# Normalizing the first block early and in two column parts, loading wk ahead of x blocks 2 and 3, and re-ranking the task order, in a fused attention + MLP kernel

## The chip, the cores and the metric

The kernel runs on one core of one Trainium2 chip. The metric is device microseconds (us) of that core. TensorE does the matrix products, VectorE (DVE in the profile) and ScalarE (ACT) the elementwise work, GpSimd (POOL) a few helpers, and SyncE (SP) issues most transfers. The profile calls TensorE "PE". The span is the stretch that the profile covers; the time is about 2 us longer than the span. A transfer has landed when its data is there. PSUM is the memory that TensorE writes its products to; it is used here in banks, which the other engines read.

## The reference, cut to what matters

```python
xn = layernorm(x)                      # x: 2048 rows of 640
return x + A(xn) + B(xn)

# A: q, k, v = xn @ wqkv; 32 heads of 20; each row looks at 8 earlier rows, 2 apart;
#    softmax over the 8; output @ wo
# B: gelu(xn @ w1 + b1) @ w2 + b2      # 640 -> 1536 -> 640
```

All operands are bf16.

## The kernel before

The rows are worked in four chunks of 512, each of four blocks of 128. The program doesn't write its instructions in a fixed order. It describes some hundreds of tasks (name, engine, modelled duration, rank, needs, buffers), and a small list scheduler runs a model of the clock: whenever an engine is free, it takes the ready task of the lowest rank. The order that comes out is the order in which each engine's queue is filled, and each engine then works its queue in that order. `RANK` holds offsets to the ranks, found by search.

```python
RANK = {
    "ad02": 53.9, "ad11": 29.1, "av2": -13.3, "f11": 8.8, ...   # cut
}
    for n, ...:                                  # n: the chunk; bl: the block in it
        pl.add(f"st{n}{bl}", VE, 1.17, ...)      # statistics, both halves and the aggregate
        pl.add(f"rs{n}{bl}", SE, 0.35, ...)      # square root        (chunk 0: by block)
        pl.add(f"rc{n}{bl}", VE, 0.17, ...)      # reciprocal
        pl.add(f"xn{n}{bl}", ...)                # normalized block: DVE in chunk 0, ScalarE later
        pl.add(f"tp{n}{bl}", PE, 0.3, ...)       # chunk 0: five transposes into a PSUM bank
        pl.add(f"tc{n}{bl}", SE, 0.65, ...)      # ... and the copy to xnT
        pl.add(f"gj{bl}{g}", PE, ...)            # chunk 0: projections block by block, 4 of 128 columns in one bank
        pl.add(f"pj{n}{which}{to}", PE, 1.08, ...)   # chunks 1 to 3: projections of 512 columns
        pl.add(f"pc{n}{which}{to}", SE, 0.52, ...)   # their copies out of PSUM (qT, kT, vT)
        pl.add(f"xs{n}", SE, 1.2, [f"at{n}"], f("xs", n), [at, ax])   # two DMA issues on ScalarE
        pl.add(f"xd{n}", DQ, 6.0, [f"at{n}"], f("xd", n), [at, ax])   # two DMA issues on SyncE
        # cut: qk, lg, max ... at (attention weights), av, ad, ot (weighted sums),
        #      f1, ge (first MLP product, gelu), o, oc (second product, output)
```

The loads are all issued by SyncE but for block 1 of x:

```python
    nc.sync.dma_start(x_sb[:, 0, :], x_nb[:, 0, :])
    nc.scalar.dma_start(x_sb[:, 1, :], x_nb[:, 1, :])
    for s in range(3):                                        # wq, wk, wv
        nc.sync.dma_start(wqkv[s][:], wqkv_v[:, :, s * D : (s + 1) * D])
        if s == 0:
            nc.sync.dma_start(x_sb[:, 2:BPC, :], x_nb[:, 2:BPC, :])
    # cut: b1, x of chunks 1 to 3, w1
```

Four transfers spread `attn` over the partitions of `ax`. Two are issued by SyncE and two by ScalarE, so they stand in ScalarE's queue among its copies:

```python
    def expand(queue, n, blocks):
        ax = get(("ax", n), lambda: axp.tile([P, BPC, W, P], BF16, tag="ax", name="ax"))
        for j in blocks:
            queue.dma_start(ax[:, j, :, :], tiles["attn", n][j * H : (j + 1) * H, :, :]...)   # cut
    def do_xd(n): expand(nc.sync, n, (0, 1))
    def do_xs(n): expand(nc.scalar, n, (2, 3))
```

`ax` has one buffer, so the issue for a chunk waits until DVE has read `ax` of the chunk before for the last time (the `pv` products). Projections and gelu inputs share four PSUM banks (tag "acc"), and a bank comes free when ScalarE (for `b1T`, DVE) has copied it out.

Names in the profile: `gps` are the projections of chunk 0, `pps` those of the later chunks, `hps` the first MLP product, `lo` and `hi` the output product, `L` the attention logits, `idle` the warm-up.

## Time and profile before

| | before |
|---|---|
| time, median of 6 runs | 215.12 us (215.06 to 216.11) |
| span of the profiled run | 212.9 us |
| TensorE busy | 206.1 us, 97% |
| first projection matmul (`gps`) | 7.70 us |
| first matmul on wk | 9.93 us |
| first `hps` matmul: all 300 projections of chunk 0 are done | 25.32 us |
| end of the last matmul | 210.10 us |

The last four rows are read from the start times in the trace. They cut the run into the start (until 25.3), the long middle, and the tail. Where holes are compared below, they are distances from one matmul's start to the next, less the usual step of that shape, with suspected missing records set aside.

### The profile page before, as it was taken

The numbers are of one execution on the slowest core, as the hardware profiler recorded it, in microseconds if no ns is written. First come the engines' busy times: TensorE is split into PE (matmuls) and PEld (weight loads), VectorE is DVE, ScalarE is ACT, GpSimd is POOL, SyncE is SP. The second block draws the span as 40 slices with busy tenths as digits, with TensorE's granted clock in tenths as the row PEclk, the third lists the DMA queues.
The fourth block names the chain that finished last, engine by engine and source line by source line (L and its number), as shares of the span: only waits on it lengthen the run. The fifth ranks groups of instructions, "written<-read, shape, count | busy, mean of one in ns | idle before, by whom it ended". The sixth has DMA issues, their size and how long they took to land.

```text
span 212.9 us, 3943 instructions
## 1 busy us (share of the span) xinstructions
PE 206.1 (97%) x1665; PEld 121.2 (57%) x1690; DVE 174.2 (82%) x176; ACT 106.8 (50%) x190; POOL 19.5 (9%) x36
## 2 busy tenths in 40 slices
PE   7899999999999999999999999999999999999994
PEld 7799844654544556556555555554555455555552
DVE  2849999459999999999999999999499789982001
ACT  3567899689565733635428273420297321351210
POOL 2000000000011015101001010110101011101220
PEclk9999999999999999999999999999999999999999
DMA  6999417973939579977002180211021822202223
GB/s 211 364 363 381 78 31 198 386 67 41 228 115 140 76 261 211 197 115 190 0 3 31 17 210 4 31 7 27 2 31 14 216 32 31 26 8 32 34 31 62
DMA packets 23433, 23.95 MB, mean 112 GB/s; under 512 B 9080, under 2 KB 20600, under 8 KB 23416
## 3 DMA queue, kind: packets, MB, share of 16 engines
q1 hardware_dynamic: 17832, 16.49, 28.0%
q0 software_dynamic: 4144, 4.92, 17.3%
q10 hardware_dynamic: 1440, 2.29, 3.7%
q8 instruction: 13, 0.21, 0.4%
q14 instruction: 4, 0.03, 0.0%
HBM read 10.00 MB, written 7.54 MB: 82 GB/s over the span
## 4 chain that ended last, share of the span: by engine, by line
PE 95%; DMA 1%; DVE 1%; issue 1%; ACT 0%
PE lo L668 26%; PE hps L637 24%; PE pps L472 23%; PE gps L489 8%; PE hi L670 8%; PE L L541 4%; DMA x_sb<-in_A_x_dram 1%; PE tp L429 0%; DVE stats L388 0%; DVE stats L389 0%; ACT xnT L433 0%; DVE xn L415 0%; DVE mv L390 0%; DVE osb L698 0%; PE b_tp L369 0%
## 5 line engine op out<-in xcount | busy, mean ns | idle before, releaser
L637 PE MATMUL hps<-xnT,w_sb 128*128 128x512 bf16 x236 | 53.9, 379 | 0.3 <-issue 0.2
L668 PE MATMUL lo<-w_sb,hT 128*128 128x512 bf16 x186 | 52.6, 379 | 0.0
L615 DVE TENSOR_TENSOR pv<-vT,ax 128x2560 bf16<-128x2560 bf16 x32 | 45.9, 1484 | 4.9 <-PE L L541 2.9
L522 DVE TENSOR_TENSOR prod<-qT,kT 128x2560 bf16<-128x2560 bf16 x32 | 45.5, 1484 | 0.0
L670 PE MATMUL hi<-w_sb,hT 128*128 128x128 bf16 x192 | 40.3, 219 | 0.3
L648 ACT ACTIVATE hT<-hps,b1T 128x512 bf16<-128x512 f32 x48 | 31.4, 687 | 17.0 <-PE hps L637 13.7
L637 PEld LDWEIGHTS <-w_sb 128*128 128x128 bf16 x240 | 22.8, 98 | 26.8 <-issue 0.4
L675 ACT CAST osb<-lo 128x512 bf16<-128x512 f32 x15 | 8.8, 585 | 50.9 <-PE hi L670 22.9
L624 DVE TENSOR_TENSOR pv<-pv 128x5120 bf16<-128x5120 bf16 x12 | 33.9, 2822 | 0.3
L668 PEld LDWEIGHTS <-hT 128*128 128x128 bf16 x192 | 18.7, 98 | 22.6 <-issue 0.2
L681 POOL DMA_DIRECT2D out_dram<-osb x15 | 12.9, 862 | 110.4 <-ACT osb L676 110.4
L668 PE MATMUL lo<-wo,oT 128*128 128x512 bf16 x74 | 22.1, 379 | 0.1
L670 PEld LDWEIGHTS <-hT 128*128 128x128 bf16 x192 | 18.4, 98 | 1.9
L670 PE MATMUL hi<-wo,oT 128*128 128x128 bf16 x80 | 16.9, 219 | 0.3
L472 PE MATMUL pps<-xnT,wk_sb 128*128 128x512 bf16 x71 | 16.9, 380 | 0.2
L472 PE MATMUL pps<-xnT,wq_sb 128*128 128x512 bf16 x72 | 16.9, 380 | 0.2
L472 PE MATMUL pps<-xnT,wv_sb 128*128 128x512 bf16 x73 | 16.9, 379 | 0.1
L689 DVE TENSOR_TENSOR osb<-lo,xlast 128x512 bf16<-128x512 f32 x1 | 0.7, 690 | 16.1 <-PE lo L668 16.1
L507 ACT CAST kT<-pps 128x512 bf16<-128x512 f32 x15 | 8.8, 584 | 8.8 <-PE pps L472 8.6
L668 PEld LDWEIGHTS <-oT 128*128 128x128 bf16 x80 | 7.8, 98 | 9.4
L472 PEld LDWEIGHTS <-wk_sb 128*128 128x128 bf16 x75 | 8.6, 118 | 7.5 <-issue 0.4
L472 PEld LDWEIGHTS <-wv_sb 128*128 128x128 bf16 x75 | 8.6, 117 | 7.2
(63 smaller groups left out, 208.2 us busy)
## 6 DMA issues: line engine op xcount, KB each, us to landing
w_sb<-in_B_w_dram SPq DMA_DIRECT2D x2, 1920.0 KB, 11.5
out_dram<-osb POOLq DMA_DIRECT2D x15, 160.0 KB, 3.4
ax<-attn SPq DMA_DIRECT2D x8, 256.0 KB, 5.1
ax<-attn ACTq DMA_DIRECT2D x8, 256.0 KB, 5.5
x_sb<-in_A_x_dram SPq DMA_DIRECT2D x3, 640.0 KB, 11.4
out_dram<-x_sb SPq DMA_DIRECT2D x3, 640.0 KB, 4.7
out_dram<-b2bc POOLq DMA_DIRECT2D x3, 640.0 KB, 7.7
wq_sb<-in_A_wqkv_dram SPq DMA_DIRECT2D x1, 800.0 KB, 4.9
```

The lines of the kernel that those rows point to most:

```text
L472: nc.tensor.matmul(ps[:], lhsT=wqkv_p[which][:, ti, to, :], rhs=xnT[:, ti, :], start=(ti == 0), stop=(ti == KT - 1),)
L489: nc.tensor.matmul(ps[:, i, :], lhsT=wqkv_p[which][:, ti, to, :], rhs=tiles["xnT", 0][:, ti, cs], start=(ti == 0), stop=(ti == KT - 1),)
L507: nc.scalar.copy(dest[:, to, off : off + CH], tiles["pps", n, which, to][:])
L522: nc.vector.tensor_tensor(out=prod[:, i, :, :], in0=qkv_tile(n, 0)[:], in1=qkv_tile(n, 1)[:, :, off : off + CH], op=ALU.mult,)
L615: nc.vector.tensor_tensor(out=pv[:, i, :, :].rearrange("p t (j c) -> p t j c", j=BPC), in0=qkv_tile(n, 2)[:, :, off : off + CH].rearrange( ...
L624: nc.vector.tensor_tensor(out=ta[:], in0=ta[:], in1=tb[:], op=ALU.add)
L637: nc.tensor.matmul(ps[:], lhsT=w1_sb[:, ti, ft * P : (ft + 1) * P], rhs=tiles["xnT", n][:, ti, :], start=(ti == 0), stop=(ti == KT - 1),)
L648: nc.scalar.activation(hT[:], tiles["hps", n, ft][:], ACT.Gelu_apprx_tanh, bias=b1T[:, ft : ft + 1], scale=1.0)
L668: nc.tensor.matmul(lo[:], lhsT=lhs, rhs=rhs[:, 0:CH], start=first, stop=last)
L670: nc.tensor.matmul(hi[:, 0 : D - CH], lhsT=lhs, rhs=rhs[:, CH:D], start=first, stop=last)
L675: nc.scalar.copy(osb[:, 0:CH], tiles["lo", n, bl][:])
L681: nc.gpsimd.dma_start(rows, tiles["osb", n, bl][:], accum_op=ALU.add)
```

## The change

The intent is to let TensorE begin sooner. Block 0's reciprocal comes ahead of block 1's second statistics; block 0 is normalized, transposed and copied in parts of 256 and 384 columns, so that its first group of projections can start on the first part; and wk, which is needed next, is loaded ahead of x blocks 2 and 3. The ranks were searched anew. The core of the diff:

```diff
-WARM = 40
+WARM = 44
 RANK = {
-    "ad02": 53.9, "ad11": 29.1, "av2": -13.3, "f11": 8.8, ...  (all 22 entries)
+    "ad02": 95.4, "av0": 25.5, "f10": 32.8, ... "rc0": 137.9, "st2": 91.4, "st3": 144.1, "xn0": -16.4,  (again 22 in all)
...
-            pl.add(f"st{n}{bl}", VE, 1.17, -40 if n else -99, [], f("st", n, bl), after=land)
+            pl.add(f"st{n}{bl}a", VE, 0.5, r, [], f("st", n, bl, 0), after=land)
+            pl.add(f"st{n}{bl}", VE, 0.62, r, [f"st{n}{bl}a"] + ([f"rc{n}{bl - 1}"] if n == 0 and bl else []), f("st", n, bl, 1))
...
+            for i, (a, b) in enumerate(((0, 2), (2, KT)) if bl == 0 else ((0, KT),)):
+                pl.add(f"xn{n}{bl}{u}", VE, ..., f("xn", n, bl, a, b), [xn])
+                pl.add(f"tp{n}{bl}{u}", PE, ..., f("tp", n, bl, a, b), [xn, tp])
+                pl.add(f"tc{n}{bl}{u}", SE, ..., f("tc", n, bl, a, b), [tp, xnT])
...
+                    if bl == 0 and g == 0:
+                        cut = 2
+                        need.append(pl.add("ga00", PE, 0.112 * tos, r, ["tc00a"], f("gj", bl, g, 0, cut), [xnT, ps], land))
...
     for s in range(3):
         nc.sync.dma_start(wqkv[s][:], wqkv_v[:, :, s * D : (s + 1) * D])
-        if s == 0:
+        if s == 1:
             nc.sync.dma_start(x_sb[:, 2:BPC, :], x_nb[:, 2:BPC, :])
...
+    zeros = consts.tile([P, P], BF16, name="zeros")
+    nc.vector.memset(zeros[:], 0.0)
...
-            nc.tensor.matmul(idle[:, 0:P], lhsT=ident[:], rhs=ident[:], start=True, stop=True)
+            nc.tensor.matmul(idle[:, 0, :], lhsT=zeros[:], rhs=zeros[:], start=True, stop=True)
```

Left out here: the task functions that take the column range, the start flag that is set once for the split group, the scheduler's modelled landing times, and the last residual add, which works in `x_sb` in place of a tile of its own.

## The prediction

> **What bounds the kernel now.** I read the page first: busy shares and the chain by engine.
>
> ```profile
> PE 206.1 (97%) x1665; PEld 121.2 (57%) x1690; DVE 174.2 (82%) x176; ACT 106.8 (50%) x190; POOL 19.5 (9%) x36
> ...
> PE 95%; DMA 1%; DVE 1%; issue 1%; ACT 0%
> ```
>
> TensorE (PE) is busy for 206.1 of 212.9 us and carries 95% of the chain, so a change helps only where it removes TensorE idle time or TensorE work. To find the idle time I asked for the busy time between the first real matmul (7.70) and the last one (210.10).
>
> ```profile
> 7.70:210.10 202.40, 200.94 (x1615) 116.48 (x1639) 170.22 (x164) 104.00 (x185) 18.21 (x19) 1.00 0.49 108
> ```
>
> The second number is the stretch, the third PE's busy time: 1.46 us idle in 202.40, spread over many small holes. After the end there are 2.8 us of tail (the last add, 0.29 us, and the store), which the change does not touch. What is left is the start, so I read the chain there, in order of time (start, length, what).
>
> ```profile
> 0.74 3.02 DMA x_sb<-in_A_x_dram
> ...
> 4.70 0.21 DVE mv L390
> 4.91 0.36 DVE stats L388
> 5.27 0.40 DVE stats L389
> ...
> 5.69 0.21 DVE mv L390
> 5.90 0.04 DVE rstd L398
> ...
> 5.96 0.46 DVE xn L415
> ...
> 6.47 0.47 PE tp L429 x5
> ...
> 6.96 0.70 ACT xnT L433
> ```
>
> Block 0 of x has landed at 3.76 and its statistics are done at 4.91. The chain then runs through the statistics of block 1 (0.36 + 0.40 + 0.21) before block 0's reciprocal. ScalarE's square root is not the holder, as its row in the timeline shows; it is over at 5.24.
>
> ```profile
> 4.95 0.29 ACT L394 ACTIVATE std<-mv,eps_t 128x1 f32<-128x1 f32 x1 [2.25 <-DVE mv L390]
> ```
>
> Last I read when the weights land (KB, us from issue to landing), because a TensorE that starts sooner asks for them sooner.
>
> ```profile
> wq_sb<-in_A_wqkv_dram SPq DMA_DIRECT2D x1, 800.0 KB, 4.9
> wk_sb<-in_A_wqkv_dram SPq DMA_DIRECT2D x1, 800.0 KB, 7.4
> ...
> x_sb<-in_A_x_dram SPq DMA_DIRECT2D x1, 320.0 KB, 5.3
> ```
>
> Their issues start at 1.20, 2.23 and 1.67 in the timeline, so wq lands at 6.10, x blocks 2 and 3 at 6.97, wk at 9.63. The first wk matmul is at 9.93, after 40 wq matmuls that fill 7.70 to 9.93 (55.7 ns each). So wk is 0.3 us early today: it is the next wait in line.
>
> **What the Trainium skill says.** "TensorE: Matmul & The Clock Gate", Part 1, says the array runs at half clock until a window of about 3.4 us was busy, and falls back after an idle window of that length; 107 ns against 56 ns for 128 columns. The trace agrees: ten warm-up matmuls take the first 1.01 us, and the real ones run at 55.7 ns from 7.70. "DMA: Bandwidth & Descriptors", Queues, rings and completion order, says each DMA engine consumes the descriptors of one queue in ring order; here wq, x 2/3 and wk land in the order of their issue. "VectorE: DVE Perf Modes", The TRN2 errata, says every instruction pays a fixed latency, so splitting costs. The trace has it for ScalarE's PSUM reads: 585 ns for 512 columns and 275 for 128 give 0.81 ns a column plus 0.17 us. "PSUM — Partial Sum Buffer", The four PSUM rules, says a start flag clears the written bits of a whole bank. That is why the split group, whose four slots share one bank, gets one start flag only; the number of matmuls stays. No run shows this yet.
>
> **The change part by part.**
>
> *Reciprocal ahead of block 1's second half.* The square root ends at 5.24, block 1's first half of statistics (start 4.83, 0.44) at 5.27. So the reciprocal can start at about 5.30 instead of 5.82, and xn at 5.44 instead of 5.96 (0.14 later, as now). Gain on this chain: 0.52.
>
> *Two column parts, 256 and 384 of 640.* A DVE operation on one column takes 0.11 to 0.15 and xn on 640 takes 0.446, so about 0.11 plus 0.52 ns a column: 0.25 and 0.31. Part a: xn 5.44 to 5.69; two transposes from 5.75 to 6.03 (one 56 ns step plus 0.219 for the last); the copy, 0.17 + 256 x 0.81 ns = 0.38, to 6.43; the first matmul at 6.47. Part b: xn until 5.95, three transposes until 6.35, its copy (0.17 + 384 x 0.81 ns = 0.48) behind part a's, 6.43 to 6.91. The 8 matmuls of part a take 8 x 55.7 ns = 0.45, until 6.92, so the 12 others follow at about 6.95. The group is through at 6.95 + 12 x 55.7 ns = 7.62. Today it is through at 7.70 + 20 x 55.7 ns = 8.81. Gain at this point: 1.19 us.
>
> *What TensorE does next.* Here I expect most of it to be lost. Block 1 is later than before: its second statistics start after xn b at about 5.95 and end at 6.67 with the aggregate; the square root waits for ScalarE's copy until 6.93, ends at 7.23; reciprocal and xn until 7.87; transposes until 8.2; copy until about 9.0. Block 0's other groups need wk. wk moves to third in the queue. From wq's 6.10, 819 KB at the 365 GB/s of these slices (the window 7.70 to 9.93 shows 369) take 2.24, so 8.34 by rate. Today's 1147 KB behind wq come 0.39 later than the same rate gives (9.63 against 9.24), so 8.3 to 8.75; I take 8.5. TensorE then stands from 7.62 to 8.5 but for block 1's five transposes (0.28), which are over before. Today the state "20 matmuls and block 1's transposes done" is reached at 8.81. What is left: 8.81 - 8.5 = 0.3 us, between 0.05 and 0.5.
>
> *x blocks 2 and 3 later.* They land at today's 9.63, as the bytes ahead of them are then the same. From 8.5 TensorE has k, q+k of block 0 (30 matmuls) and q, k, q+k of block 1 (50): 80 x 55.7 ns = 4.5 us, until 13.0, and v of both (50 more, 2.8 us) after wv's 11.84. Block 2 needs from landing to the end of its copy what block 0 needs today less its wait of 0.52: 7.66 - 3.76 - 0.52 = 3.4 us, so it is there at 13.0. Hidden, with 2.8 us of v work to spare.
>
> *Warm-up.* It waits for GpSimd's identity until 1.49; a zeroed tile on the idle DVE can be there about 0.5 us sooner (the first queues start at 0.74, small instructions take 0.1 to 0.2). 44 matmuls at 107 ns until the clock comes, then 56, end at about 5.5, against 5.75 now: free, and it keeps the array warm over the holes.
>
> *Reordered rest.* The new ranks reshuffle the matmuls after 26 us, with the same count. The 1.46 us of holes is all that they can win; a wait that they open can cost as much. I give this a gain of 0.1 with a spread of 0.5. The last add's in-place x is off the path: the DVE stood 16.1 us before the final add.
>
> Sum: 0.3 + 0.1 = 0.4 us of 215.1.
>
> **The rivals.** *The whole 1.2 us arrives.* That needs wk by about 7.6. Against it: 365 GB/s in all slices, no slack in the queue. With it: 213.8. *wk binds fully, or the hole of a microsecond at 7.6 and the idle before cools the clock.* A hole of 0.72 us today (5.75 to 6.47) does not cool it; if it happened, some 60 matmuls would take 107 instead of 56 ns, 3 us, so 218. *A new stall in the reshuffled middle or end.* DVE has 170.22 of the 202.40 us, and its last attention work ends at 193.15, only 3 us before the group of matmuls at 196.35 that reads the last oT; today the group of 190.10 holds that oT's buffer for 0.85 us. If the order delays attention by more than its slack, TensorE stands for 0.5 to 1.5 us: 215.5 to 216.5.
>
> **Range and chances.** The start gives 0.05 to 0.5, the order -1 to +1. Together 214.7, eight in ten between 213.8 and 215.5. Over 2% faster would be 4.3 us: the start's full 1.2 and all holes of 1.46 make 2.7, so 1%. Over 2% slower needs the cooled clock or a bad stall: 2%.
>
> **What would show it.** Right: reciprocal near 5.3, first projection matmul near 6.5, then a hole before the first wk matmul, which starts near 8.5 with wk's landing; the stretch from there to the last matmul nearly as long as today's. Wrong: no hole after the 20 wq matmuls (wk earlier than I worked out, or other work in between), TensorE waiting for oT or L later on, or matmuls at 107 ns after 7 us. If holes after 26 us shrink or grow by more than 0.5 us, the ranks and not the start decided.

## The result, and the profile after

The changed kernel took 216.56 us (median of 6 runs, 216.08 to 216.89), against 215.12 before. A ratio here is always the mean time of one kernel's fast runs over the mean of the other's fast runs of the same rounds, so it isn't quite the ratio of the medians. It is 1.0057, with a 95% interval of 1.0035 to 1.0080. A difference under 2% counts as "the same" here, but it is slower by about 1.2 us, outside the predicted range of 213.8 to 215.5, and on the other side of the time before than predicted.

| read from start times | before | after | difference |
|---|---|---|---|
| first `gps` matmul | 7.70 | 6.87 | -0.83 |
| first matmul on wk | 9.93 | 8.77 | -1.16 |
| first `hps` matmul | 25.32 | 25.23 | -0.09 |
| end of the last matmul | 210.10 | 211.16 | +1.06 |

So the start did begin earlier, nearly all of that was gone at 25 us, and the loss of about 1.15 us arose after it. The page of the changed kernel shows busy shares first and then the chain by engine:

```profile
PE 208.7 (98%) x1694; PEld 121.9 (57%) x1694; DVE 174.0 (81%) x178; ACT 109.3 (51%) x193; POOL 19.6 (9%) x36
...
PE 75%; DVE 16%; DMA 3%; ACT 2%; ACTq 1%; issue 1%; SPq 0%; DVEq 0%
```

TensorE's share in the chain fell from 95% to 75%. The chain now leaves TensorE somewhere and runs through DVE, a ScalarE DMA issue ("ACTq") and ScalarE before it comes back. It is not that DVE got more work (174.0 against 174.2).

**The start** is as predicted in its outline. The chain of the first 9.5 us (start, length, what) has one long piece, the landing of wk:

```profile
1.67 7.05 DMA wk_sb<-in_A_wqkv_dram
...
8.77 0.75 PE gps L505 x10
```

And the timeline there (start, length, engine, line, operation, shapes, count; in brackets the engine's idle time before it and what ended that):

```profile
4.69 0.30 ACT L406 ACTIVATE std<-mv,eps_t 128x1 f32<-128x1 f32 x1 [2.00 <-DVE mv L402]
5.02 0.16 DVE L410 RECIPROCAL rstd<-std 128x1 f32<-128x1 f32 x1
...
5.66 0.75 PE L439 MATMUL tp<-ident,xn 128*128 128x128 bf16 x5
...
6.45 0.75 ACT L443 COPY xnT<-tp 128x256 bf16<-128x256 bf16 x2 [1.46 <-PE tp L439]
6.87 1.28 PE L505 MATMUL gps<-xnT,wq_sb 128*128 128x128 bf16 x20 [0.46 <-ACT xnT L443]
...
8.13 0.45 PE L439 MATMUL tp<-ident,xn 128*128 128x128 bf16 x5
```

The reciprocal comes right behind the square root. The copy of part a starts only at 6.45, when all five transposes are through, and not after the first two. TensorE then has block 0's 20 wq matmuls and block 1's transposes, and waits 0.19 us for wk.

**The middle** is where the loss is. TensorE's list of waits (total, times, longest) of the kernel before and then of the one after:

```profile
PE tp L429 <- DVE xn L415: 0.7, 1, 0.7
PE gps L489 <- ACT xnT L433: 0.2, 1, 0.2
PE hps L637 <- issue: 0.2, 1, 0.2
```

```profile
PE pps L486 <- ACT vT L524: 0.8, 1, 0.8
PE gps L505 <- ACT xnT L443: 0.5, 1, 0.5
PE gps L505 <- DMA wk_sb<-in_A_wqkv_dram: 0.2, 1, 0.2
```

One wait is new and isn't in the start: projections of a later chunk wait 0.8 us, once, for a `vT` copy of ScalarE. ScalarE's timeline around it, in the kernel after:

```profile
80.23 0.25 ACT L531 COPY kT<-kT 128x70 bf16<-128x70 bf16 x1
81.35 2.37 ACTq L616 DMA_DIRECT2D ax<-attn  x2
83.81 1.56 ACT L524 CAST vT<-pps 128x512 bf16<-128x512 f32 x3 [3.33 <-PE pps L486]
```

and TensorE's there:

```profile
84.45 2.32 PE L486 MATMUL pps<-xnT,wv_sb 128*128 128x512 bf16 x10 [0.82 <-ACT vT L524]
```

ScalarE has its last copy done at 80.5. The next entry of its queue is not a copy but the two issues of chunk 1's `ax` transfers. They wait for DVE's last read of `ax`, which ends at 81.32, and then take 2.37 us. The first `vT` copy behind them starts at 83.81. TensorE meanwhile fills the four "acc" banks and stands: the step from the matmul before to the one at 84.45 is 1.04 us instead of 0.06, so 0.98 are lost. The bracket at 83.81 names "PE pps" as what ended ScalarE's idle time, because issuing isn't counted as busy; the line above shows what really held it.

The same issue held ScalarE as long before. ScalarE's timeline of the kernel before, and TensorE's:

```profile
91.61 0.58 ACT L507 CAST vT<-pps 128x512 bf16<-128x512 f32 x1 [0.49 <-PE pps L472]
92.89 2.34 ACTq L599 DMA_DIRECT2D ax<-attn  x2
95.27 0.58 ACT L675 CAST osb<-lo 128x512 bf16<-128x512 f32 x1 [3.08 <-PE pps L472]
```

```profile
93.58 2.32 PE L472 MATMUL pps<-xnT,wq_sb 128*128 128x512 bf16 x10
95.84 1.28 PE L541 MATMUL L<-prod,head_of 128*32 128x256 bf16 x40
```

In that order it isn't in the way: TensorE had the output product, two projection tiles and the logits to work on, which lie in other banks or in free ones, and its list of waits has none for a ScalarE copy there. So neither the transfer nor its issue is new. Only its place in the queue is.

A second, smaller hole of the same kind is at 128.8 in the kernel after (one `hps` step of 0.407 us instead of 0.216, so 0.19), behind the issue of chunk 2 at 126.07 to 128.43. The sum -0.09 + 0.98 + 0.19 is +1.08, and the end of the last matmul moved by +1.06.

### The profile page after: what moved, and what is told of

The parts are those of the page before. It is cut to its first block, busy times and chain, and to the rows that moved or that the text cites. A ratio compares the mean times of both kernels' runs of the same rounds, so it can differ in the third digit from the quotient of the medians.

```text
span 213.9 us, 3979 instructions
## 1 busy us (share of the span) xinstructions
PE 208.7 (98%) x1694; PEld 121.9 (57%) x1694; DVE 174.0 (81%) x178; ACT 109.3 (51%) x193; POOL 19.6 (9%) x36
## 4 chain that ended last, share of the span: by engine, by line
PE 75%; DVE 16%; DMA 3%; ACT 2%; ACTq 1%; issue 1%; SPq 0%; DVEq 0%
PE lo L685 27%; PE hps L654 19%; PE pps L486 11%; PE gps L505 7%; PE hi L687 7%; DVE pv L632 5%; DVE prod L539 5%; PE L L558 3%; DMA wk_sb<-in_A_wqkv_dram 3%; DVE pv L641 1%; DVE attn L606 1%; ACTq L616 1%; DVE rs L601 1%; DVE sums L596 1%; DVE sums L594 1%
## 5 line engine op out<-in xcount | busy, mean ns | idle before, releaser
L685 PE MATMUL lo<-w_sb,hT 128*128 128x512 bf16 x192 | 53.7, 379 | 0.0
L685 PEld LDWEIGHTS <-hT 128*128 128x128 bf16 x192 | 18.7, 98 | 22.7 <-issue 0.6
L685 PE MATMUL lo<-wo,oT 128*128 128x512 bf16 x80 | 23.2, 379 | 0.0
L400 DVE BATCH_NORM_STATS2 stats<-x_sb 128x6 f32<-128x320 bf16 x32 | 14.0, 469 | 5.2 <-DMA x_sb<-in_A_x_dram 5.2
L486 PE MATMUL pps<-xnT,wk_sb 128*128 128x512 bf16 x75 | 17.4, 380 | 0.0
L706 DVE TENSOR_TENSOR osb<-lo,x_sb 128x512 bf16<-128x512 f32 x1 | 0.7, 692 | 16.1 <-PE lo L685 16.1
L467 POOL DMA_DIRECT2D out_dram<-b2bc x4 | 5.3, 1334 | 88.0 <-DMA out_dram<-x_sb 88.0
```

The source lines that it names most:

```text
L400: nc.vector.bn_stats(stats[:, i, :], x_sb[:, b, i * (D // 2) : (i + 1) * (D // 2)])
L486: nc.tensor.matmul(ps[:], lhsT=wqkv_p[which][:, ti, to, :], rhs=xnT[:, ti, :], start=(ti == 0), stop=(ti == KT - 1),)
L685: nc.tensor.matmul(lo[:], lhsT=lhs, rhs=rhs[:, 0:CH], start=first, stop=last)
```

## The experiments

Every kernel gave the right result. Runs of one group share a chip and the runs of the kernel before (chip 1 in the first group, 15 in the second and third, 9 in the fourth). A comparison between groups is one across chips or rounds; the kernel before took 215.34 to 215.39 in all of them. "Holes" are worked out from start times in the trace, as above.

### First group: is it the issue on ScalarE?

My theory was the queue: the issue on ScalarE, ahead of copies that TensorE needs. The rivals were that the load order or the start does it, and that TensorE just waits for DVE. Before took 215.39 on this chip (median of 11).

**The changed kernel again**, unchanged, as the yardstick.

> The changed kernel as it is, as the control of this chip. Theory and rivals alike: 216.1 to 216.9 us, 1.004 to 1.008 of the kernel before. The trace shows a hole of 0.98 us in the matmuls near 83.4 us and one of 0.19 near 128.8.

It took 216.82 (216.59 to 217.16, 5 runs), ratio 1.0067 (1.0055 to 1.0079). The holes of 0.96 at 83.88 and 0.22 at 129.24 were there again. So was a third, of 0.61 at 14.67, which the first profile didn't have; it is taken up in the second group. The runs of the result had spans of 213.8 to 213.9 (three, the profiled one among them) and of 214.4 (three), so that this hole may sit in half of them; only e0's profile shows it.

**The issues of chunks 1 and 2 moved to SyncE:**

```diff
-        expand(nc.scalar, n, (2, 3))
+        expand(nc.sync if n in (1, 2) else nc.scalar, n, (2, 3))
```

> The changed kernel, with the two expanding DMAs that ScalarE issues in blocks 1 and 2 issued by the sync queue instead; TensorE's and DVE's order is untouched. Theory (ScalarE stands 3.3 us in its queue at those issues, and TensorE's four PSUM banks fill up meanwhile): both holes go, 0.98 + 0.19 = 1.17 us, so 215.2 to 215.5, within 0.2% of the kernel before. Rival A (TensorE waits for ScalarE's copies as such, there are too many of them there): the holes stay, 216.4. Rival B (the later landing of the expanded weights holds up DVE instead): the holes at 83 and 128 go, others come with a wait of L632 for a DMA, and the time stays above 216.

It took 215.13 (214.59 to 215.19, 6 runs), ratio 0.9985 (0.9973 to 0.9998): 1.69 us less than the unchanged one. The order of instructions on TensorE, DVE and ScalarE is the same in both traces (1694, 178 and 193 of them). The time is a little under the expected 215.2 to 215.5. ScalarE's timeline, then SyncE's and TensorE's:

```profile
80.43 0.25 ACT L531 COPY kT<-kT 128x70 bf16<-128x70 bf16 x1
81.63 1.07 ACT L524 CAST vT<-pps 128x512 bf16<-128x512 f32 x2 [0.95 <-DVE pv L632]
```

```profile
81.55 4.22 SPq L616 DMA_DIRECT2D ax<-attn  x4
```

```profile
83.66 2.32 PE L486 MATMUL pps<-xnT,wv_sb 128*128 128x512 bf16 x10
```

The four issues take SyncE 4.22 us, and nothing waits for it. The `vT` copy comes at 81.63, and the matmuls at 83.66 wait for nothing. Both holes are gone. The copy still waits 0.95 us for DVE's `pv`, which reads `vT` of two chunks ago, so it was not the wait for DVE that cost the time but the 2.4 us of issuing behind it: the rival "TensorE waits for DVE" falls.

Of the 1.69 us the span explains some 1.2 (214.4 to mostly 213.2). The other 0.5 lie outside the span; see the third group.

**The issue of chunk 1 left on ScalarE, but behind the next three `vT` copies:**

```diff
+        order = make_plan(fns).run()
+        late = order.pop([t["name"] for t in order].index("xs1"))
+        order.insert([t["name"] for t in order].index("pc222") + 1, late)
```

> The changed kernel, with ScalarE's two issues of block 1 moved in its order behind the next three copies of vT, still on ScalarE. Theory: only the place of the issue was wrong; the hole near 83.4 (0.98) closes and the one near 128.8 (0.19) stays: 215.4 to 215.7. Rival A (too many copies): the hole stays or moves by a few us, 216.4. Rival B (block 1's products wait for the transfer): DVE's first L632 of block 1 moves, 216 or more.

It took 215.58 (215.09 to 215.96, 6 runs), ratio 1.0008 (0.9992 to 1.0024), and the hole at 83 is gone, with the same issue on the same engine:

```profile
82.51 0.59 ACT L524 CAST vT<-pps 128x512 bf16<-128x512 f32 x1 [0.34 <-PE pps L486]
82.65 2.67 ACTq L616 DMA_DIRECT2D ax<-attn  x2
```

So it is its place in the queue and not that ScalarE issues. The six runs lie in two heaps, 215.1 to 215.3 (the profiled one among them) and 215.9 to 216.0; no trace of the second was taken.

**x blocks 2 and 3 ahead of wk again**, all else as changed:

```diff
-        if s == 1:
+        if s == 0:
```

> The changed kernel with the old order of the loads, x blocks 2 and 3 ahead of wk; nothing else. Theory (wk's landing ends the start, so the earlier first matmul is worth nothing by itself): the first wk matmul moves from 8.77 to about 9.7 and the time rises by 0.9 us, to 217.3, unless later holes take it up. Rival (the start does not bind, other slack hides it): no change, 216.4.

It took 217.32 (216.83 to 219.77, 6 runs), ratio 1.0107 (1.0071 to 1.0143). The first wk matmul came at 9.30, not at the expected 9.7. The direction is as expected, but the size, 0.5, is smaller than the spread of these runs (219.77 is one with a mean clock of 0.992), and in the two profiles the start ends at about the same time: the first `hps` comes at 25.76, against 25.69 in e0, which has the hole of 0.61 that this one hasn't. So this run doesn't show that the new load order helps; the fourth group comes back to it.

### Second group: the third hole, the two parts, and whether the ranks did it

Before took 215.34 on this chip (median of 11; one run at 217.62 had a mean clock of 0.992).

The third hole, in DVE's timeline of the changed kernel's second profile, with TensorE's line:

```profile
14.71 0.49 DVE L400 BATCH_NORM_STATS2 stats<-x_sb 128x6 f32<-128x320 bf16 x1 [2.18 <-DMA x_sb<-in_A_x_dram]
...
15.12 0.15 DVE L382 CAST b1T<-b_tp 128x12 f32<-128x12 bf16 x1
...
15.33 0.25 PE L505 MATMUL gps<-xnT,wq_sb 128*128 128x128 bf16 x1 [0.44 <-DVE b1T L382]
```

DVE stands 2.18 us for chunk 1's x, and only then makes the small copy `b1T`, which frees a PSUM bank that TensorE wants. In the kernel before, `b1T` was ahead of these statistics (at 12.47). In the changed kernel's first profile x landed 1 us sooner, and the same order cost nothing. That is a loss that comes and goes with a landing time.

**The issues on SyncE, and chunk 1's first statistics behind the task that makes `b1T`:**

```diff
+        first = order.pop([t["name"] for t in order].index("st10a"))
+        order.insert([t["name"] for t in order].index("gj03") + 1, first)
```

> The kernel of e1 (changed kernel, expanding DMAs of blocks 1 and 2 on the sync queue), and DVE's order altered in one place: the first half statistics of the second chunk, which wait for its x to land, are moved behind the small copy of b1. Theory: that copy frees a PSUM bank; in the changed kernel it stands behind a landing that came at 13.7 us in one profile and at 14.7 in another, where TensorE then stood 0.6 us. So the time is 215.0, up to 0.2 below e1's 215.1, and no hole appears near 14 us in any profile. Rival (the 0.6 us hole was chance and costs nothing on the mean): same as e1 within 0.1.

It took 214.88 (214.51 to 216.39, 6 runs), ratio 0.998 (0.9942 to 1.0017). The hole at 14 us is gone, but its profile has another, of 0.64 at 18.7:

```profile
19.42 0.45 PE L439 MATMUL tp<-ident,xn 128*128 128x128 bf16 x5 [0.47 <-DVE xn L426]
```

Block 3's reciprocal and `xn` stand behind all of chunk 1's statistics. It's the same fault one step later: work that waits for a late transfer is ahead of work that TensorE needs. The third group mends it.

**The same with block 0 in one part:**

```diff
     def do_xn(n, bl, a=0, b=KT):
+        if n == 0 and bl == 0:
+            if a:
+                return
+            b = KT
```

(and likewise in the transposes and the copy)

> The kernel of e4 with block 0's normalization, transposes and copy in one part again, every other instruction in its place. Theory (wk's landing ends the start, and the copy of the first part waits for all five transposes anyway): first projection matmul at about 7.2 instead of 6.9, wk's first matmul unchanged between 8.4 and 9.0, and the time within 0.1 us of e4. Rival (the two parts are what the start gains): 0.4 us slower than e4.

It took 215.78 (214.94 to 216.2, 6 runs), ratio 1.0005 (0.9968 to 1.0042), but two of the six runs, the profiled one among them, had a mean clock of 0.992. In that profile the projections from 7.3 to 10.6 us ran at 107 ns a matmul, half speed:

```profile
7.17 2.25 PE L517 MATMUL gps<-xnT,wq_sb 128*128 128x128 bf16 x20 [0.78 <-ACT xnT L455]
```

So the times say nothing about the parts; the experiment was repeated later.

**The changed kernel with the ranks of before:**

```diff
-RANK = { ... the new 22 entries ... }
+RANK = { ... the old 22 entries ... }
```

> The changed kernel with the list of ranks of the kernel before; new start, new load order and all else as changed. Theory (the ranks, not the start, cost the time): ScalarE's expanding DMAs are again behind the copies that TensorE needs, no hole above 0.3 us after 26 us, 214.9 to 215.4. Rival (the new start costs it in some other way): 216 or more.

The expectation was missed. It took 216.36 (215.41 to 217.96, 6 runs, the last with a clock of 0.992), ratio 1.0038 (0.9996 to 1.0081); two runs, at 215.41 and 215.50, lie near the expected range. A hole of 0.95 appeared, this time at 124.77, at chunk 2's issue. ScalarE's timeline, and TensorE's:

```profile
122.22 2.31 ACTq L616 DMA_DIRECT2D ax<-attn  x2
124.65 0.59 ACT L692 CAST osb<-lo 128x512 bf16<-128x512 f32 x1 [4.45 <-PE pps L486]
```

```profile
125.94 1.24 PE L486 MATMUL pps<-xnT,wv_sb 128*128 128x512 bf16 x5 [0.79 <-ACT vT L524]
```

The old ranks on the new tasks give a third order, which has the same fault in another place. So "the new ranks are bad" is too narrow: an order that lets the issue stand ahead of needed copies can pay about a microsecond, and the old ranks on the old tasks were free of it.

**The kernel before with the new ranks:**

```diff
-RANK = { ... the old 22 entries ... }
+RANK = { ... the new 22 entries ... }
```

> The kernel before with the list of ranks of the changed kernel; nothing else. ScalarE's order then has block 1's expanding DMAs between the last kT copy and the first vT copies, as in the changed kernel. Theory: a hole of about 1 us in the matmuls near 84 us, 216.2 to 216.8. Rival (the ranks are harmless with the old start): 215.1 to 215.4.

It took 216.25 (214.96 to 217.19, 6 runs), ratio 1.003 (0.9986 to 1.0074), in two heaps: three runs near 215.3 (the profiled one with a span of 213.0) and three near 217.1 (spans of 214.5 to 214.8). The median lies in the expected range, but no run does, so the expectation isn't confirmed. The profile fell into the quick heap. It holds the smaller hole at 127.9 (0.19), but at 83.36 only 0.13, because there the same two issues took 1.49 us instead of 2.37:

```profile
81.32 1.49 ACTq L599 DMA_DIRECT2D ax<-attn  x2
```

The first issue took 0.59 and the second 0.87, against 0.58 and 1.75 in the changed kernel. No profile of the slow heap was taken, so what splits the heaps isn't shown; the length of this issue is one candidate. At this place in the queue the issue doesn't always cost a microsecond.

### Third group: all three faults mended, and the rivals' own gains

Before took 215.34 (median of 13).

**The issues on SyncE, `b1T` ahead of chunk 1's statistics, and block 3's square root, reciprocal and `xn` right behind its own statistics:**

```diff
+        for name, after in (("rs03", "st03"), ("rc03", "rs03"), ("xn03", "rc03"), ("st10a", "gj03")):
+            move(name, after)
```

> The kernel of e1 (changed kernel, expanding DMAs of blocks 1 and 2 on the sync queue) with block 3's square root, reciprocal and normalization and the copy of b1 all ahead of the second chunk's statistics in the orders of ScalarE and DVE. In e4's profile TensorE stood 0.64 us at 18.7 for block 3's normalization, which stood behind those statistics, and they wait for x of the second chunk. Theory: no hole above 0.1 us between 9 and 26 us but the small ones around the b1 transpose; 214.4 to 214.8, and below e1 and e4 by 0.2 to 0.5. Rival (these holes are hidden by later waits): 214.9 to 215.2, as e1 and e4.

It took 214.46 (214.39 to 214.50, 6 runs), ratio 0.9952 (0.9919 to 0.9984), with a span of 212.5 in the profile. From the first projection on, no step of TensorE is more than 0.15 us over its usual length. It's the fastest kernel here: 2.1 us under the changed one and 0.88 under the one before (medians). Of the 0.88 only some 0.4 lie in the span (212.5 against 212.9); the rest is what the issues on SyncE gain outside it, as e10 below shows. The spread of 0.11 us is also the smallest, which fits the missing holes that came and went. Its first `hps` matmul is at 24.98, 0.34 ahead of the kernel before; the prediction had put 0.3 on the start.

**The changed kernel with old ranks, and the issues on SyncE:**

```diff
 RANK as in the kernel before
-        expand(nc.scalar, n, (2, 3))
+        expand(nc.sync if n in (1, 2) else nc.scalar, n, (2, 3))
```

> The kernel of e6 (changed kernel with the old ranks, 216.36) with the expanding DMAs of blocks 1 and 2 on the sync queue. Theory (e6 lost its time to the same wait of ScalarE, at block 2's issue near 122 us): the hole of 0.95 us near 124.8 goes, 215.2 to 215.5. Rival (e6's hole is TensorE waiting for work of ScalarE as such): unchanged, 216.3.

It took 215.14 (214.75 to 216.3, one run at clock 0.992), ratio 0.9998 (0.996 to 1.0036). The hole of 0.95 is gone. That settles the reading of the missed expectation: it was the issue there too.

**The kernel before with the issues on SyncE.** The rival: this edit might be worth something in any order, so that e1 would prove nothing about the change.

```diff
-        expand(nc.scalar, n, (2, 3))
+        expand(nc.sync if n in (1, 2) else nc.scalar, n, (2, 3))
```

> The kernel before with the same two issues on the sync queue. Theory (its order has nothing that TensorE needs behind them): no change, 214.9 to 215.4, ratio 0.999 to 1.001. Rival (issues on the sync queue are better in themselves, and e1's gain is that): 0.5% faster, 214.3.

It took 214.95 (214.73 to 215.11, 6 runs), ratio 0.9974 (0.9945 to 1.0004), so about 0.4 less; the interval just reaches 1, but all six runs lie below all 13 of the kernel before (215.16 and more). But its span is unchanged (212.8 to 213.2, against 212.9). The rival is right for 0.4 to 0.5 us, which lie outside the span, and wrong for the span. In all kernels with the issues on ScalarE, time less span is 2.2 to 2.6 us, and in all with chunks 1 and 2 on SyncE 1.9 to 2.0. I found no reason for that in the traces, and it stays open.

**The kernel before with wk first, and nothing else:**

```diff
-        if s == 0:
+        if s == 1:
```

> The kernel before with wk's load ahead of x blocks 2 and 3; nothing else. Theory: wk is not waited for there (its first matmul comes at 9.93 after 40 of wq), so nothing is won, and the transposes of blocks 2 and 3, at 11.05 in TensorE's order, now wait for statistics of x that lands at 9.6 instead of 7.0: a hole of about 1.9 us and 216.5 to 217.3. Rival (the order of loads is free there): 215.1.

It took 216.60 (216.44 to 217.44, 4 runs), ratio 1.0059 (1.002 to 1.0098). With the old order behind it, x blocks 2 and 3 come too late:

```profile
11.94 0.45 PE L429 MATMUL tp<-ident,xn 128*128 128x128 bf16 x5 [0.98 <-DVE xn L415]
```

That is the end of a hole of 1.14 that begins at 10.74, and one of 0.34 at 12.17 follows. So the load order alone loses, and needs the earlier and re-ordered start to pay.

### Fourth group: what the two parts and the load order are worth without the holes

Both start from e8, the kernel without holes, which itself wasn't run again on this chip. Before took 215.34 (median of 11).

**e8 with block 0 in one part** (the guard of e5):

```diff
+        if n == 0 and bl == 0:
+            if a:
+                return
+            b = KT
```

> The kernel of e8 (no queue holes left, runs within 0.1 us of each other, 214.46) with block 0's normalization, transposes and copy in one part, all else in its place. Theory (wk's landing at 8.4 to 9.0 ends the start): first projection matmul at about 7.2 instead of 7.0, first wk matmul unchanged, 214.4 to 214.6. Rival A (the two parts are worth their 0.4 us): 214.8 to 214.9 in all runs. Rival B (the longer pause of TensorE after the warm-up leaves its clock at half in some runs, as e5's profile showed): most runs 214.5, some at 215.5 to 216 with a mean clock of 0.992.

Five runs took 214.49 to 214.74 and one 216.5 at a clock of 0.992; median 214.50, ratio 0.9966 (0.9923 to 1.0009). Lowest against lowest is 214.49 to 214.39. TensorE's timeline:

```profile
7.19 1.28 PE L517 MATMUL gps<-xnT,wq_sb 128*128 128x128 bf16 x20 [0.78 <-ACT xnT L455]
...
8.58 1.28 PE L517 MATMUL gps<-xnT,wk_sb 128*128 128x128 bf16 x20
```

The first group starts 0.19 later than in e8 (7.19 against 7.00), but the wk group at 8.58 against 8.55, and the first `hps` at 25.01 against 24.98. At full clock the two column parts gain nothing that arrives. The second rival, about the clock, stays open: with the new start, runs at 0.992 are 3 of 12 with one part (e5 and e12) and 3 of 59 with two parts. That is too few to tell.

**e8 with x blocks 2 and 3 ahead of wk** (the edit of e3):

```diff
-        if s == 1:
+        if s == 0:
```

> The kernel of e8 with x blocks 2 and 3 loaded ahead of wk again. Theory (wk's landing ends the start): the first wk matmul moves from 8.55 to about 9.25, as in e3, and the time rises by the same 0.7 us, to 215.1 to 215.2. Rival (other slack hides it): 214.5.

It took 215.45 (215.19 to 216.63, 6 runs), ratio 1.0001 (0.9965 to 1.0037), with a span of 213.3 in the profile. Two runs, at 216.26 and 216.63, lie a microsecond above the others, and no trace shows why.

```profile
9.35 0.87 PE L505 MATMUL gps<-xnT,wk_sb 128*128 128x128 bf16 x12 [0.47 <-DMA wk_sb<-in_A_wqkv_dram]
```

The first wk matmul is at 9.35 instead of 8.55, and the first `hps` at 25.81 instead of 24.98. So within the new start the load order is worth 0.83 us there, and 0.8 in the lowest times (215.19 against 214.39). Against e12, on the same chip, it is 0.7 (214.49). It is the part of the change that carries the gain, given the earlier start: without it the first `hps` is later than in the kernel before (25.32). What the earlier reciprocal is worth by itself was not run.

## Why the prediction was right or wrong

**The step that failed** is "Reordered rest … I give this a gain of 0.1 with a spread of 0.5." It measured a loss of 1.17 in the profile (0.98 + 0.19). The new order also cost 0.61 in e0's profile, from `b1T` behind chunk 1's x at 14.67, where the step, which speaks of the matmuls after 26 us, didn't look. Two thoughts in it were wrong. The first is "The 1.46 us of holes is all that they can win": most of the 1.46 us weren't holes but missing matmul records (24 gaps of about 0.05 us, each where one step is a whole matmul longer than usual), so there was next to nothing to win. The second is its spread. It treated the order as noise around zero, and didn't ask which entries in an in-order queue wait for something late and are long themselves. The profile before held the answer: one ScalarE issue of 2.34 us with 3.08 us of idle time around it, in an engine that frees TensorE's banks, harmless only for the work that TensorE had at that moment. The scheduler's model counts this task as 1.2 us, half of what was measured, so its search had no reason to keep the task away from the copies. That the wrong model led the search there is argued, not shown.

**The rival "a new stall in the reshuffled middle or end"** was the right one, with about the right time: 215.5 to 216.5 against 216.56 measured. Its mechanism was wrong. I looked for the stall at DVE, because DVE is the second busiest engine, and at the last `oT`. It was ScalarE, which is busy 51% of the span. A busy share doesn't count issuing and says nothing of the order.

**The start, "what is left: … 0.3 us, between 0.05 and 0.5"**, held in two profiles: at the first `hps` it was 0.09 in the changed kernel's and 0.34 in e8's. Counted as the prediction does (8.81 less the first wk matmul), it was 0.04, just under the range, and 0.26. In e0's profile, with the hole at 14.67, the first `hps` was 0.37 later than before. Its core, that wk's landing takes the place of the removed wait, is right (landing at 8.72, predicted 8.5 with 8.3 to 8.75). So is the reciprocal, at 5.02 where 5.30 was predicted; the difference is that x block 0 landed 0.24 sooner (3.52). The rival "the whole 1.2 us arrives" falls for the reason given for it.

**The two column parts** were mis-stepped. I had part a's copy run from 6.05 while TensorE still transposed part b. It ran from 6.45, after all five transposes, whose last ends at 6.409 in the trace: they go into one PSUM bank, and in the trace only the fifth updates a semaphore. The transposes ran at about 107 ns a step in this profile, not 56; in e8's they ran at 56, and the copy waited for the fifth all the same. The first matmul came at 6.87 and not 6.47. Splitting had its price, as predicted: the two copies took 0.37 and 0.48, against 0.69 for the one of 640 columns before. All this cost nothing in the end, as wk bound anyway, and e12 shows that at full clock the parts could have been left out.

**x blocks 2 and 3 "hidden"** is right for the changed kernel, whose TensorE had no wait there, and e11 shows how it depends on the order: with the old one, the same load order opens 1.14 + 0.34 us.

**The warm-up** ended at 5.87 (its last matmul started at 5.55), not at the predicted 5.5, because in this profile all 44 ran at half speed; the first transpose followed at 5.66. "Keeps the array warm" was too sure. In the changed kernel's profiles the projections ran at full speed, but eight runs, of six kernels, the one before among them, have a mean clock of 0.992 and lie 0.3 to 2.5 us above the median of their kernel. What decides it isn't shown.

**The chances** were right in that the class is "within 2%". The range was wrong, because a known unknown of a microsecond was given a spread of half of it, and with the wrong sign. The prediction's last sum does say "the order -1 to +1", which with the start allows up to 216.05 (215.1 - 0.05 + 1), but its range stops at 215.5.

## What to carry to other kernels

In an engine that works its queue in order, a DMA issue is an instruction like any other: it can wait for the buffer that it fills and then hold the engine for as long as it takes (2.37 us here), and every copy behind it waits too. When an order is changed, list for each engine the entries that wait for something late, and ask which bank or buffer the entries behind them free, and whether TensorE needs it before. Where issues can stand on an engine with nothing else to do, put them there; and judge a part of a change in a kernel without stalls, since a stall elsewhere hides what it is worth.

## What the Trainium skill lacked or had wrong

- "DMA: Bandwidth & Descriptors", Issuing engines are not separate DMA queues, says that issuing on several engines only saves the sequencer's time, "which is usually small relative to the DMA itself". Here two issues of 256 KB held ScalarE for 2.37 us (0.58 and 1.75), while such a transfer takes 5.7 us from issue to landing, and cost TensorE 0.98 us. Four on SyncE took 4.22 us. The length of the second varies without a change of the transfer (0.87 in e7's profile); for this chip the page gives no time of an issue by the transfer's size or shape.
- "TensorE: Matmul & The Clock Gate", Part 1, ties the fall back to half speed to an idle window of about 3.4 us. In e5's profile matmuls ran at 107 ns from 7.3 to 10.6 us after pauses of only 0.98 and 0.78 us, though full speed had come at 3.85 us, after 27 warm-ups; in the 3.4 us between, TensorE was idle for 1.8. The page's "A second HAM failure mode" does tell of fall backs at short pauses, but gives no length. The number of cold warm-up steps varied too: 37 of 39 before, 27 of 43 in e5, all 43 in the changed kernel's profile. That agrees with the page's remark that the cold count varies from run to run.
- No page has the 0.4 to 0.5 us outside the span: time less span is 2.2 to 2.6 us where ScalarE issues the transfers of chunks 1 and 2, and 1.9 to 2.0 where SyncE does.
